# Two attention and feed-forward layers on one core: the opening is planned and placed anew

## The chip, the cores and the metric

The kernel runs on one core of a Trainium2 chip. The metric is the device time of one execution in microseconds (us). Three runs of the kernel before gave 1747.45, 1749.32 and 1751.42 us; the median, 1749.32 us, is the time before. A few figures come from one further execution that was recorded by the hardware profiler.

## The reference

```python
x = A_x                                            # 1 x 2048 x 512, bf16
x = x + _A_ref(_layernorm(x), A_wqkv, A_wo)        # attention: 32 heads of 16, full softmax
x = x + _B_ref(_layernorm(x), B_w1, B_w2)          # silu(x @ w1) @ w2, 512 -> 1792 -> 512
x = x + _A_ref(_layernorm(x), A_wqkv, A_wo)        # the same weights again
x = x + _B_ref(_layernorm(x), B_w1, B_w2)
```

The attention computes `softmax(q k^T / 4) v` over 2048 keys for each of 32 heads. The exponentials are 32 x 2048 x 2048 per layer; they are most of the work.

## The kernel before

**Units.** Scores are made in units of 128 keys by 512 queries of one head. Four heads share the TensorE array in row groups of 32 (`KT0` holds the keys of the first four, `KT1` of the next four, and so on; both come from one matmul group of a pair, `k_seq`). Scores go into two PSUM tiles in turn, `s3` of three banks and `s2` of two. ScalarE (ACT) exponentiates a whole tile in one instruction (`p<-s`). Where a bank and VectorE (DVE) are free, the planner gives a further unit to DVE (`spare`), which computes the exponential in four instructions (`v`, then three on `e`). `p` or `e` is then multiplied with V and a column of ones (`vaug`), which gives numerator and denominator together.

**A planner writes the order.** The program is made by a list scheduler that runs while the kernel is built. `Machine` keeps a model of the clock of each engine: `submit` queues an operation of ACT, DVE or SP with its cost; `track` finds what it depends on; `choice` picks the next one of an engine (priority -1 ahead of 0 ahead of 1, and an operation of higher priority is waited for by a fraction of a microsecond); `pump` emits all that begins before a given time; `pe` books a matmul. What is emitted stays in program order on its engine, so the model's times decide the order on the chip, but only semaphores decide when an instruction really starts. The tile framework (the follower of the program's order) adds those semaphores.

**The main loop** (in `stream`) tries at each step, in this order: scores (`emit_s`) if a score tile is free and its inputs are there; products with V (`pv_step`); a step of other matmuls (`fill_step`) from the lanes of `order()`; a dummy matmul (`dummy`). Dummies keep TensorE's clock up: one is made when the model's TensorE was busy for less than 0.66 (`FLOOR`) of the last 3.42 us (`WINDOW`).

**The opening.** The layer norm statistics of the first 1024 tokens are split between ACT and DVE. The lanes are `prep` (normalize a tile of 128 tokens into a `p` buffer), `turns` (transpose it on TensorE, copy it to `xt` by ACT or DVE, whichever the model has free first), `firsts` (keys of the first pair for two chunks of 512 tokens, then its early queries) and `values` (V tiles, `v_seq`). Eight tiles are turned so; the other eight are turned by DMA once scores run.

The early queries need a bound on the scores: the greatest absolute key of each row (`amaxp`, one reduction per chunk, then `amax`), put into the small matrices `E` by DVE, and `|q|` (`qa`). The matmul of `E` and `qa` subtracts the bound; its result is cast to `qt`, and then the first scores can be made. The names of the steps are thus, in order: `p` (normalized tile), `xt` (transposed), key matmuls, `amaxp`, `KT`, query matmuls, `qa`, `amax`, `E`, the matmul of `E` and `qa`, `qt`, scores `s`, exponential `p<-s`.

**Banks.** `g0` to `g2` (banks 0 to 2) live for the whole kernel. Banks 3 to 7 are `x0` to `x4` in the opening; at the first scores their pool is closed (`open_slots`), and `s3` takes banks 3 to 5, `s2` banks 6 and 7. Before the change a step in the opening takes whichever of the eight banks the model has free first, but once the query steps have begun, and always for those, only the first three. `slot_time` says when a score tile's banks are free, and scores are held while any of banks 3 to 7 is being filled.

**Around the exponential table.** ACT starts with the table set that has the square root. The first use of `Exp` loads another (`ACT_TABLE_LOAD`). Before the change a dummy `Exp` stands behind the first `qa`, which ACT computes with `Abs`. After the scores have begun (`started`), `qa` is always made by DVE.

**The end.** The last 256 tokens of the second layer can't be overlapped with more exponentials; `end_tokens` runs them with dummies of its own (`warm(11, ...)`) while their layer norm is computed.

In the profile most of ACT's, DVE's and TensorE's instructions carry the line of one of three helpers (L280, L419, L423), so they are told apart by the names of their tiles. Dummies are matmuls with `ident` as weights and `x_sb` as moving operand.

Of the kernel before, what the change touches and what calls it, by code (L numbers as in the profile page):

```python
# [10 lines left out]
ALU = mybir.AluOpType  # L11
# [21 lines left out]
class Machine:  # L33
# [13 lines left out]
    def __init__(self, tc):  # L47
        self.tc, self.on = tc, False
        self.regions, self.cache, self.grain = {}, {}, {}
        self.free = {"ACT": 0.0, "DVE": 0.0, "SP": 0.0}  # L50
        self.pending = {"ACT": [], "DVE": [], "SP": []}
        self.rows = [0.0] * 4
        self.mode, self.floor = None, 0.0
        self.busy = []

    def spans(self, ap):
# [32 lines left out]
    def track(self, op, reads, writes):  # L89
        deps = {}  # L90
        for ap in reads:
            known = self.regions.setdefault(ap.name, {})
            for w, _ in self.overlapping(ap):
                if w is not None:
                    deps[w] = 1
            for lo, hi in self.spans(ap):
                mine = known.setdefault((lo, hi), [None, []])
                if op.eng == "PE":
                    mine[1][:] = [o for o in mine[1] if o.eng != "PE"]
                mine[1].append(op)  # L100
        for ap in writes:
            known = self.regions.setdefault(ap.name, {})
            for lo, hi in self.spans(ap):
                for (a, b), (w, rs) in list(known.items()):
                    if a < hi and lo < b:
                        if w is not None:
                            deps[w] = 1
                        deps.update(dict.fromkeys(rs))
                        if lo <= a and b <= hi:
                            del known[a, b]  # L110
                known[lo, hi] = [op, []]
        deps.pop(op, None)
        return deps
# [110 lines left out]
    def pe(self, mode, row, cols, reads, writes, fn):  # L224

        op = Op("PE", 0.0, 0.0, (), None, 0)
        op.deps = self.track(op, reads, writes)
        if not self.on:
            op.end = 0.0
            return fn()  # L230
        for d in list(op.deps):
            self.force(d)
        if mode != self.mode:
            base = self.begins(mode)
            self.rows, self.mode = [base] * 4, mode
        rows = range(4) if row is None else (row,)
        self.floor = max(self.floor, self.ready(op))
        at = max(self.floor, *(self.rows[r] for r in rows))
        end = at + cols * self.COL
        for r in rows:  # L240
            self.rows[r] = end
        op.end = end + self.SEEN
        op.deps = ()
        if self.busy and at <= self.busy[-1][1] + 0.001:
            self.busy[-1][1] = max(self.busy[-1][1], end)
        else:
            self.busy.append([at, end])
        ins = fn()
        return self.tc.keep_in_program_order(ins)
# [48 lines left out]
class Seq:  # L298


    def __init__(self, steps, bank=True, when=None, lock=None, taken=None):
        self.steps, self.bank, self.when, self.lock, self.taken = steps, bank, when, lock, taken
        self.at, self.own = 0, None

    @property
# [40 lines left out]
def kernel(  # L346
# [106 lines left out]
    def bank_time(i):  # L453
        return INF if shut[i] else M.released(banks[i][:])

    def best_bank(every=True):
        return min(range(len(banks) if opening[0] and every else 3), key=bank_time)

    def take_bank(every=True):
        i = best_bank(every)  # L460
        assert not shut[i]
        shut[i] = True
        return i
# [167 lines left out]
    def k_seq(L, pr, c, when=None):  # L631

        def step(ct):
            def fn(g):
                mm(
                    g[:, :],
                    lhsT=wk_sb[:, ct, P * pr : P * (pr + 1)],
                    rhs=L.xnT[c][:, ct, :],
                    start=(ct == 0),
                    stop=(ct == CT - 1),  # L640
                )
                if ct < CT - 1:
                    return
                V.tensor_reduce(
                    out=amaxp[pr][:, c : c + 1], in_=g[:, :], axis=AX.X, op=ALU.max,
                    apply_absolute_value=True, prio=0 if started[0] else -1,
                )
                for par in range(2):
                    dst = KT[2 * pr + par][:, c * 512 : (c + 1) * 512]
                    if not started[0] and par == 0:  # L650
                        A.activation(
                            dst, g[:, :], ACT.Identity, bias=onescol[par], scale=headcol[par]
                        )
                    else:
                        V.tensor_scalar(
                            out=dst, in0=g[:, :], scalar1=headcol[par], scalar2=onescol[par],
                            op0=ALU.mult, op1=ALU.add, prio=0 if started[0] else 1,
                        )
                    L.k_made.add((2 * pr + par, c))
                used_xt(L, c)  # L660

            return fn

        return Seq([(step(ct), 512, lambda: [L.xnT[c][:]]) for ct in range(CT)], when=when)

    def v_seq(L, tt, cost=512, when=None):
        c = tt // 4

        def step(ct):
            def fn(g):  # L670
                at = tt % 4 * P
                mm(
                    g[:, :],
                    lhsT=L.xnT[c][:, ct, at : at + P],
                    rhs=wv_sb[:, ct, :],
                    start=(ct == 0),
                    stop=(ct == CT - 1),
                )
                if ct < CT - 1:
                    return  # L680
                dst = L.vaug[:, tt, 0 : 17 * H].rearrange("p (h e) -> p h e", e=17)[:, :, 0:DH]
                src = g[:, :].rearrange("p (h d) -> p h d", d=DH)
                L.v_made[tt] = evict(dst, src, 0 if started[0] else 1)
                used_xt(L, c)

            return fn

        return Seq([(step(ct), cost, lambda: [L.xnT[c][:]]) for ct in range(CT)], when=when)

    def new_vaug(n):  # L690
        vaug = keep([P, TT, VW], BF16, f"vaug{n}")
# [8 lines left out]
    def q_seq(L, c, pr, early=False, which=(0, 1), when=None):  # L700
# [3 lines left out]
        def step(ct):  # L704
            def fn(g):
# [29 lines left out]
                        )  # L735
                if ct < CT - 1:
                    return
                if not started[0]:
                    A.activation(qa[:], g[:, :], ACT.Abs)
                    if pr == 0:  # L740
                        M.submit(
                            "ACT", 1.5, 0.1, [qa[:]], [lnt[:, 0:1]],
                            lambda: nc.scalar.activation(lnt[:, 0:1], onescol[0], ACT.Exp),
                        )
                else:
                    V.tensor_scalar(
                        out=qa[:].bitcast(U16),
                        in0=g[:, :].bitcast(U16).rearrange("p (n h) -> p n h", h=2)[:, :, 1],
                        scalar1=0x7FFF, scalar2=None, op0=ALU.bitwise_and,
                    )  # L750
                used_xt(L, c)

            return fn
# [12 lines left out]
        def inputs(i):  # L766
# [3 lines left out]
        return Seq(  # L770
            steps + [(last(i), 512, inputs(i)) for i in range(len(which))],
            when=lambda: len(qt_ring.tiles) >= len(which) and (when is None or when()),
            lock="qa",
        )

    def drop_q(L, key):
# [358 lines left out]
    def stream(layers, before, values, side, last, second_half):  # L1135
# [295 lines left out]
        def step_of(lane, tp, ready=True):  # L1431


            if not lane.seqs:
                return None
            s = lane.seqs[0]
            if s.at == 0:
                if s.when is not None and not s.when():
                    return None
                if s.lock in Lane.locks:  # L1440
                    return None
                if s.bank and bank_time(best_bank(not s.lock)) > (tp + 0.02 if ready else 1e12):
                    return None
            if ready and M.written(*s.steps[s.at][2]()) > tp + 0.02 + (
                M.SWITCH if M.mode != "F" else 0.0
            ):
                return None
            return s

        def do_step(lane):  # L1450
            s = lane.seqs[0]
            if s.at == 0:
                if s.lock:
                    Lane.locks.add(s.lock)
                if s.bank:
                    s.own = take_bank(not s.lock)
            fn, cost, _ = s.steps[s.at]
            s.at += 1
            done = s.at == len(s.steps)
# [96 lines left out]
            return any(kt not in b.L.v_made for kt in range(k, n))  # L1556

        def fill_step(tp, s_at):
            urgent = not waiting or lacking() or short_of_v() or any(
                x[2].end is not None and x[2].end < tp - 2.0 for x in todo[:1]  # L1560
            )
# [104 lines left out]
    for at, t in (  # L1666
# [2 lines left out]
    ):  # L1669
        M.arrive(at, t)  # L1670
    M.free.update(ACT=4.0, DVE=2.5)
    M.WAIT = M.WAIT | {-1: 0.4}
    M.on = True
    HALF, ON_ACT = TT // 2, slice(3, 8, 4)
# [74 lines left out]
    def first_turn(tt):  # L1749
        c, tq = divmod(tt, 4)  # L1750

        def fn(g):
# [2 lines left out]
            dst = L1.xnT[c][:, :, tq * P : (tq + 1) * P]  # L1755
            if tt < HALF:
                to_transposed(room[tt], dst, g)
            else:
                by_dma(room[tt], dst)
            turned[c] += 1  # L1760
# [66 lines left out]
```

## Time and profile before

| | us |
|---|---|
| median of three runs | 1749.32 |
| profiled execution | 1750.5 |
| its span, first to last instruction | 1748.7 |
| ACT busy (98% of the span) | 1713.8 |
| DVE busy (93%) | 1629.3 |
| TensorE busy, matmuls (90%) | 1575.7 |
| first exponential of scores starts at | 21.49 |
| last exponential of scores starts at | 1723.40 |

The profile gives for each instruction its engine, line, operation and the tiles that it writes and reads (`out<-in`), its start and duration. In the timeline neighbouring instructions of a kind are merged: start, time from the start of the first to the end of the last, engine, line, operation, tiles, shape, count, and in brackets how long the engine had been idle before and on what it waited. PEld are TensorE's weight loads, which run beside the matmuls. A matmul's recorded time includes its way through the array, so the distance between neighbouring weight loads says better how fast TensorE works.

### The profile page before, as it was taken

How to read it: one execution, taken by the hardware profiler on the slowest of the kernel's cores; microseconds unless marked ns; L12 is line 12 of the kernel's file. 1: busy time of each engine (PE TensorE's matmuls, PEld its weight loads, DVE VectorE, ACT ScalarE, POOL GpSimd, SP SyncE). 2: the span in 40 equal slices, each digit the busy share in tenths (PEclk: the TensorE clock that was granted, in tenths of full speed). 3: DMA queues.
4: the chain of work that ended last, by engine and by line, in shares of the span. 5: the costliest groups of instructions: out<-in, count | busy, mean ns of one | idle time of the engine just before them, and what ended most of it. 6: DMA issues, size and time to landing. Idle time of an engine off the chain costs nothing.

```text
span 1748.7 us, 32237 instructions
## 1 busy us (share of the span) xinstructions
PE 1575.7 (90%) x12733; PEld 533.1 (30%) x12733; DVE 1629.3 (93%) x3165; ACT 1713.8 (98%) x1610; POOL 6.6 (0%) x20
## 2 busy tenths in 40 slices
PE   8899998999989999999989888989999898889988
PEld 2222222222222223334322222222222222333444
DVE  8999999999998999999999985979999999998995
ACT  8999999999999999999999999999999999999996
POOL 1000000000000000000000000000000000000000
PEclk9999999999999999999999999999999999999999
DMA  5100011000100001010010000100001000100100
GB/s 184 34 10 7 13 19 19 7 16 7 20 16 7 19 4 33 4 26 12 12 17 13 10 7 19 31 6 17 7 7 28 7 19 4 21 18 12 25 14 13
DMA packets 98088, 33.41 MB, mean 19 GB/s; under 512 B 89488, under 2 KB 97424, under 8 KB 97936
## 3 DMA queue, kind: packets, MB, share of 16 engines
q1 hardware_dynamic: 97936, 31.35, 8.2%
q8 instruction: 99, 1.62, 0.4%
q14 instruction: 53, 0.43, 0.1%
HBM read 7.86 MB, written 2.10 MB: 6 GB/s over the span
## 4 chain that ended last, share of the span: by engine, by line
ACT 44%; DVE 21%; PE 16%; issue 15%; DMA 3%; ACTq 0%; DVEq 0%
ACT p L280 41%; PE g L419 10%; DVE e L280 9%; PE s L419 5%; DVE v L280 4%; ACT t_sb L280 3%; DMA o<-oT 3%; DVE KT L280 2%; DVE hT L280 1%; DVE qt L280 1%; DVE amaxp L280 1%; DVE oT L280 1%; DVE vaug L280 0%; DVE qa L280 0%; DVE attn L280 0%
## 5 line engine op out<-in xcount | busy, mean ns | idle before, releaser
L280 ACT ACTIVATE p<-s 128x1536 bf16<-128x1536 f32 (+1 forms) x1446 | 1671.1, 1410 | 11.7 <-PE s L419 7.7
L419 PE MATMUL s<-qt,KT 32*128 32x512 bf16 (+1 forms) x4512 | 569.4, 339 | 108.8 <-ACT p L280 90.1
L419 PE MATMUL g<-p,vaug 128*32 128x512 bf16 (+1 forms) x4512 | 479.2, 344 | 17.8 <-ACT p L280 15.6
L419 PEld LDWEIGHTS <-KT 32*128 32x128 bf16 x5128 | 209.6, 91 | 623.2 <-issue 605.0
L280 DVE TENSOR_SCALAR v<-g 128x512 f32<-128x512 f32 x481 | 328.1, 682 | 23.8 <-PE g L419 18.6
L280 DVE SCALAR_TENSOR_TENSOR e<-e,v 128x512 uint16<-128x512 bf16 x481 | 325.4, 680 | 0.6
L280 DVE SCALAR_TENSOR_TENSOR e<-v,e 128x512 bf16<-128x512 uint16 x481 | 325.0, 680 | 0.7
L280 DVE SCALAR_TENSOR_TENSOR e<-v 128x512 bf16<-128x512 uint16 x481 | 322.5, 681 | 0.8
L419 PE MATMUL g<-wo_sb,ident 128*128 128x512 bf16 x681 | 210.6, 385 | 7.8 <-DVE v L280 5.3
L419 PEld LDWEIGHTS <-vaug 128*32 128x32 bf16 x5120 | 141.7, 95 | 220.5 <-issue 208.0
L419 PE MATMUL g<-qt,KT 32*128 32x512 bf16 (+1 forms) x608 | 185.4, 338 | 1.5 <-DVE KT L280 1.1
L419 PE MATMUL g<-e,vaug 128*32 128x512 bf16 (+1 forms) x608 | 173.0, 343 | 5.2 <-DVE e L280 2.5
L419 PE MATMUL g<-w_sb,hT 128*128 128x512 bf16 x448 | 131.2, 384 | 0.9 <-DVE hT L280 0.8
L419 PE MATMUL g<-xt,w_sb 128*128 128x512 bf16 x336 | 100.2, 387 | 9.3 <-DVE hT L280 6.5
L280 DVE SCALAR_TENSOR_TENSOR hT<-t_sb,g 128x512 bf16<-128x512 f32 x105 | 71.2, 678 | 21.2 <-ACT t_sb L280 20.9
L419 PEld LDWEIGHTS <-ident 128*128 128x128 bf16 x703 | 52.7, 98 | 112.3 <-issue 98.6
L280 ACT ACTIVATE t_sb<-g 128x512 f32<-128x512 f32 x105 | 82.4, 784 | 0.6 <-PE g L419 0.3
L280 DVE CAST oT<-g 128x512 bf16<-128x512 f32 (+1 forms) x94 | 55.6, 592 | 23.0 <-PE g L419 22.7
L419 PEld LDWEIGHTS <-hT 128*128 128x128 bf16 x568 | 41.8, 97 | 87.4 <-issue 69.7
L419 PEld LDWEIGHTS <-w_sb 128*128 128x128 bf16 x560 | 45.1, 98 | 68.9 <-issue 56.6
L280 DVE CAST qt<-g 128x512 bf16<-128x512 f32 x78 | 53.0, 680 | 2.9 <-PE g L419 2.8
L419 PE MATMUL g<-xt,wq_sb 128*128 128x512 bf16 x160 | 50.4, 390 | 1.9 <-DVE v L280 0.9
(128 smaller groups left out, 636.5 us busy)
## 6 DMA issues: line engine op xcount, KB each, us to landing
w_sb<-in_B_w_dram SPq DMA_DIRECT2D x2, 1792.0 KB, 13.9
x_sb<-in_A_x_dram SPq DMA_DIRECT2D x4, 512.0 KB, 7.0
out_dram<-x_sb SPq DMA_DIRECT2D x7, 256.0 KB, 2.1
o<-oT SPq DMA_TRANSPOSE x93, 2.4
xt<-hT SPq DMA_TRANSPOSE x48, 2.3
wk_sb<-in_A_wqkv_dram SPq DMA_DIRECT2D x1, 512.0 KB, 6.4
wq_sb<-in_A_wqkv_dram SPq DMA_DIRECT2D x1, 512.0 KB, 7.3
wv_sb<-in_A_wqkv_dram SPq DMA_DIRECT2D x1, 512.0 KB, 8.3
```

What stands on the lines that cost most here:

```text
L280: return self.m.submit(self.name, pitch, tail, aps, outs, lambda: fn(*args, **kw), prio)
L419: lambda: nc.tensor.matmul(out, lhsT=lhsT, rhs=rhs, **kw),
```

## The change

It has four parts, all of them in the opening or in the planner's picture of it.

1. The model books a matmul that begins before 10.4 us (`warm`) at 1.96 times its cost. Of the matmuls before that time only dummies are concerned.
2. `track` makes a read of a PSUM tile by ACT or DVE depend on earlier reads of it by the other of the two. This is in the model; the instructions and the semaphores of the tile framework are not changed by it, only the order of emission.
3. Keys and queries take banks 0 to 2, V tiles banks 6 and 7 until the score tiles exist, and banks 0 to 2 then. While scores have not begun, a filling step is not started if scores are due within 0.35 us.
4. The first `qa` is made by DVE, as the later ones are, and the dummy `Exp` stands behind the transposed copy of the eighth tile.

```diff
@@ Machine.__init__
-        self.mode, self.floor = None, 0.0
+        self.mode, self.floor, self.warm = None, 0.0, 0.0
@@ Machine.track, for each tile that is read
             for w, _ in self.overlapping(ap):
                 if w is not None:
                     deps[w] = 1
+            if op.eng != "PE" and ap.space == bass.MemoryType.PSUM:
+                for _, rs in self.overlapping(ap):
+                    deps.update((o, 1) for o in rs if o.eng not in (op.eng, "PE"))
@@ Machine.pe
-        end = at + cols * self.COL
+        end = at + cols * self.COL * (1.0 if at >= self.warm else 1.96)
@@ Seq.__init__
-    def __init__(self, steps, bank=True, when=None, lock=None, taken=None):
+    def __init__(self, steps, bank=True, when=None, lock=None, where=None):
@@ banks
-    def best_bank(every=True):
-        return min(range(len(banks) if opening[0] and every else 3), key=bank_time)
-
-    def take_bank(every=True):
-        i = best_bank(every)
+    def best_bank(where=None):
+        if s_slots or where is None and not opening[0]:
+            where = range(3)
+        return min(where or range(len(banks)), key=bank_time)
+
+    def take_bank(where=None):
+        i = best_bank(where)
@@ k_seq, v_seq, q_seq: what their Seq is given
+        k_seq: where=range(3)      v_seq: where=(6, 7)      q_seq: where=range(3)
@@ q_seq, after the last query matmul
-                if not started[0]:
-                    A.activation(qa[:], g[:, :], ACT.Abs)
-                    if pr == 0:
-                        M.submit(
-                            "ACT", 1.5, 0.1, [qa[:]], [lnt[:, 0:1]],
-                            lambda: nc.scalar.activation(lnt[:, 0:1], onescol[0], ACT.Exp),
-                        )
-                else:
-                    V.tensor_scalar(
-                        out=qa[:].bitcast(U16),
-                        in0=g[:, :].bitcast(U16).rearrange("p (n h) -> p n h", h=2)[:, :, 1],
-                        scalar1=0x7FFF, scalar2=None, op0=ALU.bitwise_and,
-                    )
+                V.tensor_scalar(
+                    out=qa[:].bitcast(U16),
+                    in0=g[:, :].bitcast(U16).rearrange("p (n h) -> p n h", h=2)[:, :, 1],
+                    scalar1=0x7FFF, scalar2=None, op0=ALU.bitwise_and,
+                )
@@ step_of, do_step
-                if s.bank and bank_time(best_bank(not s.lock)) > (tp + 0.02 if ready else 1e12):
+                if s.bank and bank_time(best_bank(s.where)) > (tp + 0.02 if ready else 1e12):
...
-                    s.own = take_bank(not s.lock)
+                    s.own = take_bank(s.where)
@@ fill_step
+            if not started[0] and s_at < tp + 0.35:
+                return False
@@ beginning of the planned part
     M.free.update(ACT=4.0, DVE=2.5)
+    M.warm = 10.4
@@ first_turn
             if tt < HALF:
                 to_transposed(room[tt], dst, g)
+                if tt == HALF - 1:
+                    M.submit(
+                        "ACT", 1.5, 0.1, [dst], [lnt[:, 0:1]],
+                        lambda: nc.scalar.activation(lnt[:, 0:1], onescol[0], ACT.Exp),
+                    )
```

## The prediction

> **What bounds the kernel now.** I began with the page: its span and its busy lines say which engine is full, and the slices say where it is not.
>
> ```profile
> span 1748.7 us, 32237 instructions
> PE 1575.7 (90%) x12733; PEld 533.1 (30%) x12733; DVE 1629.3 (93%) x3165; ACT 1713.8 (98%) x1610; POOL 6.6 (0%) x20
> ```
>
> ScalarE (ACT) is busy for all but 34.9 us. Where those 34.9 us lie is answered by the table of stretches (columns: length, then busy time of PE, PEld, DVE, ACT, POOL):
>
> ```profile
> 0.00:21.49 21.49, 15.31 (x83) 7.07 (x83) 13.90 (x44) 14.19 (x34) 6.58 (x20) 1.00 0.95 323
> 21.49:60.00 38.51, 35.38 (x228) 9.82 (x227) 37.91 (x92) 37.91 (x34) 0.00 (x0) 1.00 0.23 59
> ...
> 1726.00:1748.70 22.70, 17.88 (x108) 10.45 (x108) 9.69 (x18) 6.59 (x10) 0.00 (x0) 0.90 0.04 12
> ```
>
> 7.3 us lie before the first exponential at 21.49, 16.1 us in the tail, and 11.5 us are spread over the 1704.5 us between. So the time is: start (21.49) + ACT's queue, nearly without a hole, + tail (22.7). A change of the beginning moves the total by what it moves the first exponential, one for one, and beyond that only through what it does to the length of ACT's queue. The third view is the timeline of the opening:
>
> ```profile
> 10.23 1.23 PEld L419 LDWEIGHTS <-ident 128*128 128x128 bf16 x6 [0.28 <-issue]
> ...
> 11.79 0.83 PE L423 MATMUL x<-ident,p 128*128 128x128 bf16 x12
> 12.21 1.56 ACT L280 COPY xt<-x 128x512 bf16<-128x512 bf16 x3 [1.35 <-PE x L423]
> ...
> 16.88 0.81 DVE L280 TENSOR_SCALAR KT<-x,cols 128x512 bf16<-128x512 f32 x1 [0.85 <-ACT KT L280]
> ...
> 17.46 0.60 ACT L280 ACTIVATE qa<-g 128x512 bf16<-128x512 f32 x1
> 17.60 0.68 DVE L280 TENSOR_REDUCE amaxp<-g 128x1 f32<-128x512 f32 x1
> ...
> 18.07 1.28 ACT L743 ACT_TABLE_LOAD   x1
> ...
> 19.67 0.68 DVE L280 CAST qt<-g 128x512 bf16<-128x512 f32 x1
> ...
> 20.27 0.68 DVE L280 CAST vaug<-x 128x512 bf16<-128x512 f32 x1
> ...
> 21.00 0.39 PE L419 MATMUL s<-qt,KT 32*128 32x512 bf16 x3 [0.61 <-DVE vaug L280]
> ...
> 21.49 9.15 ACT L280 ACTIVATE p<-s 128x1536 bf16<-128x1536 f32 x8 [0.94 <-PE s L419]
> ```
>
> To be seen: PE still works off dummies until 11.58, though the first normalized tile was there at 9.69 + 0.35 = 10.04; DVE's KT stands 0.85 behind ACT's read of the same bank, and amaxp of the second key chunk stands behind that, though its matmuls (15.54 to 16.56) were long done; the first scores wait 0.61 for a V eviction after qt. Each of the four parts of the change goes at one of these.
>
> **Dummies at the cold rate.** The 20 dummies before the transposes (20 weight loads of ident) are issued 0.43 apart until 10.23 and 0.216 apart after (six loads in 1.23). The planner booked all of them at 0.218, so its PE clock ran ahead of the chip's. With 0.218 x 1.96 = 0.427 each and the unchanged rule (fill 0.66 of 3.42 us = 2.26 us), I count by hand: six dummies from 4.8 to 7.4, none until the first slides out of the window at 8.6, four more to 10.3, where the tile is due: 10 in place of 20. On the chip nothing holds PE in the planned gap, so they end at 4.73 + 10 x 0.427 = 9.00. The transposes then start when the tile lands, at about 10.15, not 11.58: 1.43 gained on PE. ACT can't use all of it: its own p and a sel run to 10.87 (10.59 + 0.28), so its copies start at 10.87, not 12.21: 1.34. From there by the rows: 1.56 for three copies, 0.52 for the fourth, 0.77 for four small constants, 0.60 for the last copy: 14.32, where it was 15.49. The second chunk's key matmuls follow at 14.4 and end at 15.3 (they took 0.86 of issue from 15.54 to 16.40).
>
> **Readers of a bank in a row.** The model now makes a read of a PSUM tile wait for earlier readers on other engines, which is what the 0.85 shows the chip doing. It adds no instruction. DVE will be given amaxp of chunk 1 before KT of chunk 0. It can start at 15.3 + 0.2 = 15.5, not 17.60. From amaxp to the last E operation took 17.60 to 19.04, 1.44, so E stands at 16.94 and not 19.04: 2.1 of lead. Elsewhere the rule binds nothing new: after the opening DVE alone reads key banks, and tanh's bank has its ACT reader ahead of DVE's already through t_sb.
>
> **Abs moves to DVE, the exp table moves ahead.** qa was ACT's 0.60 at 17.46, beside DVE's work. On DVE it takes 0.68 (the other 39 qa average 681 ns) and now stands in the row behind E, since the E operations have the higher priority: 16.94 to 17.62. That is the full 0.68 on the path. Queued behind it: KT of the odd head (0.81 each, twice) and V evictions. The table load (1.28, with its dummy activation 0.20) goes behind the last copy, 14.32 to 15.80; KT of both chunks on ACT follow to about 17.3 (0.78 and 0.68 of pitch). That is 1.8 ahead of the new qt, so the load costs nothing; if that cover were gone it would cost at most its 1.48. In the old place it cost nothing either: ACT idled for 0.94 before its first exponential. No second load is expected, as ACT went from exp to vaug's cast and back at 19.96 to 21.49 without one.
>
> **qt and the first scores.** The E matmul (0.39) runs from 17.65 to 18.05; DVE, free at 17.62, will fill the wait with a KT (0.81), to 18.43; qt follows to 19.1, the scores start at 19.15, and the exponential 0.49 later: 19.65. Against 21.49 that is 1.84 earlier.
>
> **V tiles in banks 6 and 7.** Before, one V eviction in an x bank held the scores for 0.61. The trace can't show whether the scores' new tile waits for all five old banks or only for the three it covers. Bounds: 0.6 gained if the wait goes; 0.7 lost if a second eviction (0.68) stands in front. My chain to 19.65 has no such wait; in the row's own order, an eviction right behind qt, it comes back at 0.6: 20.25. I take the middle, 19.9, since V tiles still sit in banks that the score tiles take over, and ACT, idle after 17.3, can take some of the evictions: the start moves by 21.49 - 19.9 = 1.6. The new guard (no filling step within 0.35 us of the scores) and the fixed sets of three banks for keys and queries add no work; they can delay a V tile, whose first reader comes 3.3 us behind the scores (24.34 against 21.00).
>
> **The rest of ACT's queue.** Eight exponentials of 20 units in 9.15 us make 0.46 us a unit. DVE takes 481 of the units (the costliest groups of the page: four instructions of 0.68 each). Every unit that changes sides moves the end by 0.46. What DVE brings over the start (two KT, 1.6 us, less than one unit's 2.7) is worth 0.3. But the planner places every later step anew from the shifted state. DVE's idle time between 60 and 1726 is about 99 us, so its time does not fix the split; free banks and the backlog rule do. The profile excludes neither sign: I take zero, and as bounds 8 units either way (3.7 us, one in sixty of the 481). The tail has one more term. Its eleven dummies run at half clock:
>
> ```profile
> 1727.23:1730.64 3.41, 3.35 (x8) 1.19 (x9) 2.04 (x8) 1.94 (x4) 0.00 (x0) 0.50 0.00 0
> ```
>
> The transposes behind them start at 1731.53, where their input (first of two writes in 0.73 from 1730.28) was there at about 1730.7: 0.8 can come back if the slow stretch falls elsewhere, and as much or 1.7 (half of 3.41) be lost if it falls on the hidden matmuls. I take zero.
>
> **Sum.** The profiled execution took 1750.5 (span 1748.7 and 1.8 around it): 1750.5 - 1.6 = 1748.9. The median of the runs shown is 1749.3, so there the same step gives 1747.7.
>
> **Rivals.**
> The start moves and the split or the tail falls kindly: 1.6 + 7 units x 0.46 = 4.8, or 1744.5. For it: 99 us of idle DVE. Against: nothing in the change aims there. 0.22.
>
> More units stay on ACT, and the end is slower. Mechanism: at the start DVE now owes two KT and the V evictions, its backlog is over the 3.0 us at which the planner offers it no unit, and the order that follows finds a bank free less often. Each lost unit costs 0.46; from four the gain of 1.6 is gone, at twelve (2.5% of 481) it is +3.9: 1753.2. For it: DVE is 98% busy between 21.49 and 60 (37.91 of 38.51), so there is nothing to catch up with. Against: that stretch is 2% of the span. 0.15.
>
> The clock stays low. Ten dummies fill 4.3 us where twenty kept PE busy up to the transposes, and PE then idles from 9.0 to 10.15. In this run 5.5 us of unbroken dummies were needed (4.73 to 10.23). If 4.3 do not do, the four key, four key, four query matmuls and the E matmul run at 0.427 in place of 0.216, 13 x 0.21 = 2.7, while the transposes (0.26 a tile, then 0.5) still hide behind copies of 0.52. The start is then 1.1 later than before: 1750.4. It decides itself at the weight loads after 10.2. 0.13. The Trainium skill, TensorE: Matmul & The Clock Gate, Part 1, says that full clock is granted after one busy window of some 3.4 us on a free-running grid, and Part 4 that transposes don't count as busy in the same way; by that rule ten dummies suffice for most positions of the grid and fail for some, and the trace's 5.5 us agree with a grid, since its first window was only partly filled. That the rule speaks against thinner dummies is why I do not leave this rival out.
>
> **How the numbers follow.** The forecast, 1747.7 with the rest of the queue unmoved, has 0.50. What a measurement of this kernel can tell from no change is about 0.2%, 3.5 us. Faster by more: the kind rival 0.22 and 0.04 from the forecast's edge; slower by more: the unkind one 0.15 and 0.01 of the cold clock; between lie 0.58. The range reaches 4.8 + 1 below and 2.9 above the median: 1743.5 to 1752.2.
>
> **What would show it.** Right: 10 or 11 weight loads of ident before the transposes, these at 10.1 to 10.3; amaxp of the second chunk ahead of any DVE KT; qa on DVE right behind E; the table load between the last xt copy and ACT's KT; first exponential between 19.3 and 20.3; the count of v on DVE within 8 of 481. Wrong: loads of wk_sb 0.43 apart after 10.3, ACT idle between its KT, scores still waiting for vaug, or an end that moves by other than the start did.

## The result

The changed kernel took 1745.14 us (median of 13 runs, 1741.14 to 1748.49), the kernel before 1748.25 us beside it (13 runs, 1744.97 to 1751.59). The ratio is 0.9974, 95% interval 0.9964 to 0.9984: faster by 0.26%, which is 4.5 us of 1748. The ratio compares the means; the two medians are 3.1 us apart. In a second set of runs on another chip the ratio was 0.9951 (0.9936 to 0.9967).

The page of the changed kernel's profiled execution (1745.14 us):

```profile
span 1743.4 us, 32282 instructions
...
PE 1568.3 (90%) x12750; PEld 530.6 (30%) x12750; DVE 1630.2 (94%) x3168; ACT 1713.3 (98%) x1611; POOL 6.6 (0%) x20
```

The span is 5.3 shorter; ACT's work is the same to 0.5 us. The table of stretches is cut at this kernel's first scores (19.57) and behind its last exponential (1719.73 to 1720.53). It gives the length, then the busy time of PE, PEld, DVE, ACT and POOL, the mean granted clock, and the share and rate of the DMA:

```profile
0.00:19.60 19.60, 12.37 (x74) 5.92 (x74) 13.24 (x44) 14.47 (x35) 6.56 (x20) 1.00 0.94 319
19.60:60.00 40.40, 38.49 (x245) 10.88 (x244) 39.91 (x96) 39.53 (x35) 0.00 (x0) 1.00 0.28 74
...
1722.00:1743.40 21.40, 16.51 (x108) 9.99 (x108) 9.56 (x18) 6.46 (x10) 0.00 (x0) 0.97 0.04 12
```

From the instructions' times of the two profiles: the first exponential starts at 20.06 (before 21.49, 1.4 earlier), the time from the first to the last one is 1699.67 (before 1701.91, 2.2 shorter), and from there to the end it is 23.6 (before 25.3, 1.7 shorter). So the start carries a quarter of the profiled gain. Units on DVE: 482 (before 481). Between the start of the first and the end of the last exponential ACT was idle for 9.6 us (before 11.4) and busy for 1690.9 (before 1691.8). The opening in the timeline:

```profile
10.38 1.52 PEld L426 LDWEIGHTS <-p 128*128 128x128 bf16 x20 [2.12 <-DVE p L283]
...
11.13 1.52 ACT L283 COPY xt<-x 128x512 bf16<-128x512 bf16 x3
...
14.38 1.28 ACT L1765 ACT_TABLE_LOAD   x1
...
15.58 0.69 DVE L283 TENSOR_REDUCE amaxp<-g 128x1 f32<-128x512 f32 x1 [0.68 <-PE g L422]
...
15.78 1.43 ACT L283 ACTIVATE KT<-g,cols 128x512 bf16<-128x512 f32 x2
...
16.91 0.69 DVE L283 TENSOR_SCALAR qa<-g 128x512 uint16<-128x512 uint16 x1
...
17.51 0.80 DVE L283 TENSOR_SCALAR KT<-g,cols 128x512 bf16<-128x512 f32 x1
...
18.23 0.68 DVE L283 CAST qt<-g 128x512 bf16<-128x512 f32 x1
...
18.93 0.59 ACT L283 CAST vaug<-x 128x512 bf16<-128x512 f32 x1 [0.68 <-PE x L422]
...
19.57 0.39 PE L422 MATMUL s<-qt,KT 32*128 32x512 bf16 x3 [0.68 <-ACT vaug L283]
...
20.06 4.62 ACT L283 ACTIVATE p<-s 128x1536 bf16<-128x1536 f32 x4 [0.55 <-PE s L422]
```

To be seen: PE now waits 2.12 for the first normalized tile, where that tile had waited for PE; the second amaxp stands ahead of every KT; qa follows E on DVE, a KT fills the wait before qt, and the scores still wait 0.68 for a V eviction, now ACT's.

Where the rest came from shows when the finished units (ACT's and DVE's together, 4096) are counted in both traces. The changed kernel leads by 1.4 us at unit 3, trails by 2.5 at unit 2048 (870 us), trails by 0.2 at unit 2304 (981 us), and leads by 5.4 at unit 2816 (1203 us). That one step of 5.6 us is more than the whole gain between the first and the last exponential (2.2); elsewhere the changed kernel loses ground, 3.9 us up to unit 2048 and 1.7 behind unit 2816. In that stretch the second layer takes over. Its groups, first before, then after (mean of one, idle time ahead of them and who ended it):

```profile
L280 ACT ACTIVATE p<-s 128x1024 bf16<-128x1024 f32 (+1 forms) x187 | 217.4, 1368 | 3.9 <-PE g L419 2.4 <-PE s L419 1.2
```

```profile
L280 DVE TENSOR_SCALAR v<-g 128x512 f32<-128x512 f32 x49 | 33.4, 682 | 5.1 <-PE g L419 4.5
```

```profile
L283 ACT ACTIVATE p<-s 128x1536 bf16<-128x1536 f32 (+1 forms) x186 | 215.3, 1464 | 0.4 <-PE g L422 0.4
```

```profile
L283 DVE TENSOR_SCALAR v<-g 128x512 f32<-128x512 f32 x53 | 36.4, 686 | 1.8 <-PE g L422 1.5
```

ACT stood for 3.9 us there before and for 0.4 after, and DVE took 53 units instead of 49: 3.5 + 4 x 0.46 = 5.3, which is about the step from 0.2 behind to 5.4 ahead. Nothing in the change aims at this place. The step is not one execution's: the six other profiles of the changed opening, from the experiments below, have it too (5.0 to 7.0 us, with at most 0.9 us of such holes and 52 or 53 units on DVE). Of ACT's holes in the kernel before, 2.3 us lie in two stretches of half clock, at 1027.5 and 1143.6; whether the clock made them or the same sparse work made both is not shown.

The tail's eleven dummies now run at full clock, issued in 2.26 us, where the eleven loads of before went from 1727.69 to 1731.42:

```profile
1723.35 2.26 PEld L422 LDWEIGHTS <-ident 128*128 128x128 bf16 x11
```

### The profile page after: what moved, and what is told of

It is laid out like the page before. It is cut to its first block, busy times and chain, and to the rows that moved or that the text cites. A ratio compares the mean times of both kernels' runs of the same rounds, so it can differ in the third digit from the quotient of the medians.

```text
span 1743.4 us, 32282 instructions
## 1 busy us (share of the span) xinstructions
PE 1568.3 (90%) x12750; PEld 530.6 (30%) x12750; DVE 1630.2 (94%) x3168; ACT 1713.3 (98%) x1611; POOL 6.6 (0%) x20
## 4 chain that ended last, share of the span: by engine, by line
ACT 50%; DVE 19%; issue 16%; PE 12%; DMA 3%; ACTq 0%; SPq 0%; DVEq 0%
ACT p L283 46%; DVE e L283 8%; PE g L422 7%; PE s L422 4%; DVE v L283 4%; ACT t_sb L283 3%; DMA o<-oT 3%; DVE KT L283 1%; DVE hT L283 1%; DVE oT L283 1%; DVE amaxp L283 1%; DVE qt L283 1%; DVE qa L283 0%; DVE x_sb L283 0%; DVE attn L283 0%
## 5 line engine op out<-in xcount | busy, mean ns | idle before, releaser
L422 PE MATMUL g<-p,vaug 128*32 128x512 bf16 (+1 forms) x4514 | 476.5, 343 | 14.1 <-ACT p L283 13.0
## 6 DMA issues: line engine op xcount, KB each, us to landing
w_sb<-in_B_w_dram SPq DMA_DIRECT2D x2, 1792.0 KB, 14.1
```

The costliest lines, as they stand in the source:

```text
L422: lambda: nc.tensor.matmul(out, lhsT=lhsT, rhs=rhs, **kw),
```

## The experiments

Ratios are to runs of the kernel before in the same set, with 95% intervals. "First exponential" is from the one profiled execution of each; x lands at 4.7 to 5.0 in them, except where noted. "From landing" counts the same from where x lands; a star marks profiles in which TensorE's clock was at half for some of the work between the dummies and the first scores. "At equal clock" is an estimate: the time in us above or below the kernel before on the same chip, with both brought to the same mean granted clock by one straight line through all 194 runs that list a clock (-920 us for the whole of the clock); the 95% intervals of its entries are 0.7 to 1.1 us either way. It also takes out what a kernel itself does to the clock.

| kernel | ratio | first exponential | from landing | units on DVE | at equal clock |
|---|---|---|---|---|---|
| changed kernel, first set | 0.9974 (0.9964 to 0.9984) | 20.06 | 15.12 | 482 | no clocks for before |
| changed kernel, again | 0.9951 (0.9936 to 0.9967) | 20.88 | 16.13* | 482 | -6.0 |
| 24 late matmuls | 0.9947 (0.9932 to 0.9962) | 23.30 | 18.59 | 482 | -6.6 |
| 24 early matmuls | 0.9930 (0.9912 to 0.9947) | 20.92 | 16.17* | 482 | -9.5 |
| x lands late | 0.9979 (0.9964 to 0.9995) | 23.23 | 15.22 | 482 | -2.6 |
| changed, placed with 0.201 | 0.9961 (0.9946 to 0.9976) | 21.61 | 16.72* | 481 | -5.8 |
| changed, placed with 0.199 | 0.9963 (0.9949 to 0.9977) | 20.09 | 15.19 | 482 | -6.6 |
| before, placed with 0.201 | 0.9987 (0.9976 to 0.9999) | 20.59 | 15.86 | 483 | -1.2 |
| part 1 alone | 1.0007 (0.9994 to 1.0019) | 22.25 | 17.36* | 480 | 0.8 |
| part 4 alone | 0.9951 (0.9934 to 0.9968) | 19.93 | 15.14 | 484 | -6.2 |
| parts 1, 3, 4 | 1.0003 (0.9991 to 1.0015) | 20.74 | 15.99 | 483 | -2.8 |
| parts 1, 2, 4 | 1.0002 (0.9990 to 1.0014) | 20.09 | 15.37 | 480 | -0.4 |
| parts 1, 2, 3 | 1.0052 (1.0033 to 1.0070) | 21.17 | 16.52* | 476 | 1.1 |

**Is the end moved by what the start is moved?** First the changed kernel again, and with 24 matmuls in front of the first transposes that the planner doesn't book.

> The changed kernel once more, as the ruler for the other runs of this set. The theory that the first exponential's lead is all (1.6 us of 1748) expects 0.9991 of the kernel before; the theory that the order placed anew behind the start gave about as much again expects 0.997 to 0.998, as on record.

> The changed kernel with 24 matmuls more in front of the first transposes that the planner does not know of: the order of everything else is that of the changed kernel, only the start comes later, by 4 to 7 us (24 at 0.216 to 0.427 from where the ten dummies end, less the 1.1 us in which PE was idle). Theory one for one (ACT's queue has no hole that could take up a late start): the end comes later by what the first exponential comes later, 4 to 7 us, within 1 us. Rival (engines have slack and catch up): less than half of that arrives at the end, 0 to 3 us.

```diff
+            if tt == 0:
+                for _ in range(24):
+                    tc.keep_in_program_order(
+                        nc.tensor.matmul(
+                            g[:, :], lhsT=ident[:, :], rhs=x_sb[:, 0, :], start=True, stop=True
+                        )
+                    )
             if tt < HALF:
                 to_transposed(room[tt], dst, g)
```

The start came 2.4 to 3.2 later (23.30; 4 to 7 had been expected), and the time was the same: medians 1743.09 and 1743.26. As it stood, the rival had won. The instructions of ACT and DVE and their order are the same in both. But the two traces, instruction by instruction, keep the 3.24 unchanged from the first exponential to 66 us and lose it later at separate places. DVE's wait for `o`, a tile that SP transposes by DMA, was one of them: at 294.6 DVE waited 1.2 in the changed kernel and not in the late one.

```profile
L628 SPq DMA_TRANSPOSE o<-oT x93: 1168/1190/2427, 38.0 to 1711.5; - x93
```

Most transposes are issued in 1.19 us, some in up to 2.4. All long ones (over 1.5: 10 of 179 in the changed kernel, 7 in the late one) have a packet of the instruction queue between 1.5 us ahead of their issue and 2.6 behind it; of all 179, 60 and 54 have, so most with such a packet are not long. The additional matmuls change which ones are long: counted in their order on SP's queue, 9 of the changed kernel's 10 long ones are long again in its second profile and 8 with late data (below; TensorE's stream is the same), but none of them with 24 matmuls more; the late and the early run share 5 of their 7 and 8. So the 24 additional matmuls did two things: they delayed the start, and they moved everything behind them in TensorE's instruction stream, after which other transposes were long. Two runs separate these.

> The changed kernel with the 24 unplanned matmuls put where TensorE waits for x anyway (128 columns, before 4.7 us) instead of in front of the transposes: TensorE's stream is as long as in the run with 24 late matmuls, and all that follows stands at the same place in it, but the start is not delayed (first exponential near 20, not 23.3). Theory that the late run took its 2.4 to 3.2 us back because its longer stream meets fewer slow transposes and weight-clock stretches: 1740 to 1741, 2.4 to 3.2 below the late run. Rival (the start's time does not reach the end): 1743, like the late run.

```diff
     M.on = True
+    for _ in range(24):
+        tc.keep_in_program_order(
+            nc.tensor.matmul(
+                banks[1][:, 0:P], lhsT=ident[:, :], rhs=ident[:, :], start=True, stop=True
+            )
+        )
```

> The changed kernel with the loads of wk and wq put ahead of the first loads of x: no engine's instructions or their order change, but x lands some 2 to 3.5 us later (two loads of 512 KB more ahead of it) and with it the whole opening. Theory one for one: the end comes 2 to 3.5 us later than that of the changed kernel, as the first exponential does. Rival from the run with 24 late matmuls (a late start is taken up by slack behind it): the end moves by under 1 us.

```diff
+    def load_w(w, at):
+        nc.sync.dma_start(w[:], A_wqkv[:, at : at + D].rearrange("(ct p) f -> p ct f", p=P))
+
+    load_w(wk_sb, D)
+    load_w(wq_sb, 0)
     load_x(0)
     load_x(1)
-    for w, at in ((wk_sb, D), (wq_sb, 0), (wv_sb, 2 * D)):
-        nc.sync.dma_start(w[:], A_wqkv[:, at : at + D].rearrange("(ct p) f -> p ct f", p=P))
+    load_w(wv_sb, 2 * D)
```

With a stream of the same length and no delay, the first exponential came 2.38 earlier than in the late run (20.92), and the ratio is 0.9930 against 0.9947: 0.17%, 3.0 us, for 2.4 of start. With an unchanged stream and x landing at 8.01 instead of 4.75 to 4.95, the first exponential came 2.4 to 3.2 later (23.23), and the ratio is 0.9979 against 0.9951: 0.28%, 4.9 us. These ratios are from different sets, each to the kernel before beside it, and the interval of such a difference is some 0.22% either way. So the first pair fits one for one and doesn't exclude nothing; the second excludes nothing and fits one for one. Together they give 0.23% (0.15% either way) for about 2.6 us of start, or 0.15%. But the second pair hangs on which ratio of the changed kernel is taken: with the 0.9974 of the first set, 0.05% is left. By the ratios alone the rival is not out.

The clocks settle it. At equal clock, late data costs 3.3 us (1.3 either way) and the late run is 2.9 (1.5 either way) behind the early one: both exclude nothing and fit one for one. The profiles agree: between the changed kernel and late data, which have the same instructions of ACT and DVE in the same order, the first exponential moves by 3.17 and the span by 3.19, though their distance wanders between 2.0 and 5.0 in the middle; between the early and the late run it is 2.38 and 2.81.

What the longer stream gave by itself is the early run against the changed kernel with the same start (20.92 and 20.88): 0.9930 against 0.9951, 3.7 us; their intervals overlap a little, but at equal clock it is 3.5 us (1.5 either way). That its cause is the transposes was seen at single places and not isolated. The early run has the lowest ratio of all; it beats the kernel before clearly and the changed kernel by that margin.

**What does placing anew give?** A single constant of the model is moved by 1 ns from the first scores on.

> The changed kernel with one constant of the model changed from the first scores on (a matmul's result is taken to be seen after 0.201 instead of 0.200 us): the opening is the same, all that follows is placed anew. Theory that where the planner happens to place things decides some us: the end moves by up to 3 us either way against the changed kernel though the start does not. Rival (placing anew is worth nothing): within 1 us of the changed kernel.

> As the run with 0.201, with 0.199: a second draw of the order behind the same start. The same two theories: up to 3 us either way, or within 1 us of the changed kernel.

> The kernel before with the model's constant at 0.201 from the first scores on: the same opening, all behind it placed anew. Theory that what the change gained beyond its start is a draw of the placement, and that the kernel before has a slow draw: 3 to 6 us below the kernel before. Rival (the changed opening leaves a state that is better to go on from): within 1.5 us of the kernel before.

```diff
     def second_half():
         halves_asked[1] = True
+        M.SEEN = 0.201      # 0.199 in the other run
```

DVE's order leaves the changed kernel's at 878 us (0.201) and at 164 us (0.199), that of the kernel before at 630 us. The changed opening gave 0.9961 and 0.9963, the old one 0.9987: differences of the order of 0.1% by 1 ns, upward behind the new opening and downward behind the old. Those of the new opening are within the intervals (the medians are 2.1 and 2.6 us above the changed kernel's, and at equal clock the three are within 0.8 us), so neither of their two theories is out. The old opening's second draw came 2.3 us (0.13%) lower, not 3 to 6 and not within 1.5, but its interval, 0.2 to 4.2 us, reaches into both ranges. Three draws behind the new opening lie lower than two behind the old one. Whether this holds of the opening or of five draws stays open; below, two kernels with most of the new opening do not lie lower by the ratio.

One of these profiles also shows a rival of the prediction at work. The opening's order is the changed kernel's, yet its first exponential is 1.55 later (21.61). The columns are those of the table of stretches:

```profile
9.00:12.50 3.50, 2.11 (x24) 1.29 (x24) 3.03 (x12) 3.47 (x12) 0.00 (x0) 1.00 1.10 348
12.50:15.90 3.40, 3.40 (x18) 1.92 (x17) 1.29 (x4) 2.47 (x7) 0.00 (x0) 0.50 1.09 375
```

The clock (column behind POOL) was full, and after a stretch in which PE was busy for 2.11 of 3.50, mostly with transposes, it fell to half for 3.4 us. Such a stretch doesn't always cost the clock: in the changed kernel's first profile PE was busy for 1.78 of the 3.41 us from 7.99, in the one with 0.199 for 2.27 of the 3.41 from 9.52, and the clock stayed full. What decides it stays open. In the early run it fell at 11.0, and in the second run of the changed kernel, by the spacing of its weight loads (0.4 up to 13.81), it was not full before 14.1. Counted from x's landing, the first exponential of this opening came at 15.12, 15.19 and 15.22 in three profiles at full clock and at 16.13, 16.17 and 16.72 in these three. The old opening has two profiles, 15.86 (full clock from 8.5) and 16.78 (from 10.3).

**Which part does it?** One part alone, then all but one.

> The kernel before with the first part alone (dummies booked at the cold rate). Theory of the prediction: the transposes start 1.3 us earlier and the first exponential 1.0 to 1.4 earlier than 21.5; the end by the same, with up to 3 us of placement either way. Rival (the clock stays low with ten dummies): transposes 0.107 apart and a first exponential no earlier than 21.5.

The diff is part 1 of the change on the kernel before. The transposes started 1.6 earlier from x's landing (5.51 against 7.08), and the first exponential came later than before, 22.25:

```profile
16.28 0.78 ACT L280 ACTIVATE KT<-g,cols 128x512 bf16<-128x512 f32 x1 [1.00 <-DVE amaxp L280]
18.53 0.78 ACT L280 ACTIVATE KT<-x,cols 128x512 bf16<-128x512 f32 x1 [1.48 <-DVE amaxp L280]
```

The time is the rival's, but the clock did not stay low with ten dummies: it was full from 8.9 and fell to half from 12.3 to 15.8. The lead is also lost behind DVE's readers (ACT's two KT wait 1.00 and 1.48 for amaxp). How much each took is not separated; the changed kernel with 0.201, at half clock in the same place, has 16.72 from x's landing against 17.36 here. The end did not move measurably.

> The kernel before with the fourth part alone (first qa on DVE, exp table behind the last transposed copy). Theory of the prediction: by itself it costs, 0.7 us of qa on DVE's row in front of qt and up to 1.5 of table load in front of ACT's KT: first exponential at 22 to 23. Rival (moving the load off the place in front of the first scores is where the change gains): first exponential at 20.0 to 20.5.

Part 4 on the kernel before. First exponential 19.93, ratio 0.9951: the rival's direction, just under its range. From x's landing that is 15.14, and 0.72 earlier than the old opening at full clock (15.86). The table load does not cost its 1.48, it re-orders:

```profile
14.70 1.28 ACT L1753 ACT_TABLE_LOAD   x1
...
16.10 0.76 ACT L280 ACTIVATE KT<-x,cols 128x512 bf16<-128x512 f32 x1
```

```profile
15.14 0.80 DVE L280 TENSOR_SCALAR KT<-x,cols 128x512 bf16<-128x512 f32 x1
15.86 0.68 DVE L280 TENSOR_REDUCE amaxp<-g 128x1 f32<-128x512 f32 x1
```

While ACT loads the table, DVE reads the first chunk's bank for its KT ahead of ACT, with no wait of 0.85, and the second amaxp follows at 15.86. Which half of part 4 did it, the load's place or qa on DVE, was not run apart.

> Parts one to three without the fourth: qa stays on ACT, the exp table load behind it. Theory of the prediction: qa no longer stands in DVE's row, so the first exponential comes up to 0.7 earlier than in the changed kernel, 19.3 to 20.0. Rival (from the run of part four alone): the load of 1.28 then stands in front of ACT's V evictions, which hold the scores, and the first exponential comes at 20.7 to 21.5.

Parts 1 to 3. First exponential 21.17, in the rival's range:

```profile
18.75 0.68 DVE L283 CAST qt<-g 128x512 bf16<-128x512 f32 x1
19.34 1.28 DVE L283 CAST vaug<-x 128x512 bf16<-128x512 f32 x2
```

```profile
20.68 0.39 PE L422 MATMUL s<-qt,KT 32*128 32x512 bf16 x3 [2.31 <-DVE vaug L283]
```

ACT loads its table from 17.97 to 19.25, so two V evictions go to DVE behind qt and the scores wait for them. The clock has a share too: it was not full before 13.3, and qt starts 0.8 later from x's landing than in the changed kernel (14.10 against 13.28). The end is 0.52% later, much more than the start. DVE took 476 units, and ACT stood idle for 20.1 us between the first and the last exponential, 13.5 of them in stretches of half clock (4.95 in one wait at 378, in a stretch of 10.24). The mean granted clock of these runs is 0.985, that of the kernel before 0.994; at equal clock only 1.1 us of 9 are left.

> Parts one, three and four, without readers of a bank kept in a row in the model. Theory of the prediction: amaxp of the second key chunk falls behind KT's readers again, and the first exponential comes 1 to 2 us later than in the changed kernel, 21 to 22.5. Rival (from the run of part four alone): the early table load by itself puts ACT's KT behind amaxp, and the first exponential stays at 20 to 20.6.

Parts 1, 3 and 4:

```profile
15.52 0.81 DVE L280 TENSOR_SCALAR KT<-g,cols 128x512 bf16<-128x512 f32 x1 [0.84 <-ACT KT L280]
16.25 0.68 DVE L280 TENSOR_REDUCE amaxp<-g 128x1 f32<-128x512 f32 x1
```

KT waits 0.84 for ACT's read again and the second amaxp comes behind it. From x's landing the first exponential is 0.87 later than in the changed kernel (15.99 against 15.12), near the theory's lower end; 20.74 by the span lies between the two ranges.

> Parts one, two and four, without banks of their own for V tiles and without the guard. Theory of the prediction (V tiles sit in banks that the score tiles take over either way): first exponential as in the changed kernel, 19.9 to 20.6. Rival (the banks take a wait of 0.6 away): 20.7 to 21.3.

Parts 1, 2 and 4: 20.09, as the theory had it; the banks of their own move the start by 0.25 from x's landing (15.37 against 15.12). So parts 1, 2 and 4 have nearly the changed kernel's start and no gain at the end (1.0002); parts 1, 3 and 4 have lost the new start (15.99, against 15.86 of the old opening at full clock) and gain nothing either (1.0003).

## Why the prediction was right, and where not

The direction and the range held (1745.14 in 1743.5 to 1752.2); the range ran from 5.8 us below the kernel before to 2.9 above and so held no change too: to lie inside it says little. The direction came right in good part for another reason than the forecast's, since parts 1, 2 and 4 have the start and no gain. The size was under-estimated: 0.26% is 4.5 us, and 1.6 was forecast. The time of the rival in which split and tail fall kindly (1744.5) is what came; it had 0.22. Its mechanism came in part: the tail was kind, but the split moved by one unit and not by seven. Two of the signs that the prediction named as wrong came too: the scores still wait for vaug, and the end moved by other than the start (5.4 against 1.4 in the profiles).

**Dummies: right in the order, over-priced in the gain.** Ten matmuls, the last one done at 8.76 (forecast 9.00), transposes at 10.39. With x landing 0.24 later in this profile, the copies (forecast 10.87, measured 11.13) stand where they were put, and the steps behind them come close: second amaxp 15.5 and 15.58, qa 16.94 and 16.91, qt 18.43 and 18.23, exponential 19.9 and 20.06. But the start of the old opening was read from one profile, whose clock became full only at 10.3. Its transposes began 7.08 from x's landing; in the two other profiles with the old dummies (before with 0.201, part 4 alone), full from 8.5 and 8.6, they began at 6.16 and 6.20, and in those with ten dummies at 5.42 to 5.53. So about 0.9 of the 1.43 that the prediction gained on PE was that one profile's late clock.

**V tiles: the middle was taken, and the whole wait stayed,** 0.68, now for ACT. That the exponential still came where it was forecast is luck: from x's landing, qt started 0.44 earlier than forecast (13.28 against 13.72), which made up for it.

**The table load at no cost: right for the sum, wrong for what it does.** The two profiles agree that it is hidden. But part 4 alone gives the whole start (15.14 from landing, the changed kernel 15.12 to 15.22 at full clock) and the whole gain at the end (-6.2 us at equal clock, the changed kernel -6.0), and without it the scores wait 2.31 for V evictions. The prediction priced where the load stands on ACT and not what DVE does in the meantime, nor that in its old place it would drive V evictions onto DVE once the scores come earlier.

**The clock: the chance of 0.13 was far too low.** In three of six profiles of this opening the clock was at half in the middle of it. The price was over-estimated: 1.0 to 1.5 against the mean of the other three, not 2.7, since one stretch at half clock covers only a part of the matmuls that the rival counted. Ten dummies fill 4.27 us, so they cover a whole 3.41 us from end to end for only a quarter of its possible places (0.86 of 3.41), not for most as the prediction put it; yet in seven of the nine profiles with ten dummies alone (not in the changed kernel's second one and in parts 1 to 3) the clock became full from them, in the first one from a stretch (4.58 to 7.99) in which they began 0.4 late. So the start was mis-sized too: over the profiles at hand it moves by about 0.6 (means 15.76 of six and 16.32 of two from x's landing), at full clock by 0.7, not 1.6. That the two profiles on which prediction and result rest show 1.43 is luck of their clocks. The Trainium skill, TensorE: Matmul & The Clock Gate, Part 1, gives a busy window of some 3.4 us on a free-running grid as the condition for full clock; the half-clock stretches of 3.4 us and their changing places agree with that. The table of the same part lets the clock fall after an idle window; here it fell, in the run shown above, with no gap over 1.13 (9.26 to 10.39) and transposes behind it, and the measurement decides. That transposes count for less, which the prediction took in, is not borne out by parts 1 to 3: there the clock became full at 13.29, after 3.41 us in which PE was busy for 3.13 and worked off 24 transposes and one other matmul.

**The rest of the queue taken as zero: the term that was mis-sized most.** Between 981 and 1203 us it gave 5.3, and over the kernels whose first exponential comes within 1 us of the changed one's the ratio ranges from 0.9930 to 1.0003, 13 us. The bound of 8 units (3.7 us) covered only the split; ACT's own holes were left out of it. Between the first and the last exponential they make 4.8 us (early run) to 20.1 (parts 1 to 3) in the fourteen profiles, while ACT's work there differs by 5.2. Why an order has fewer holes was not isolated.

**Tail: the 0.8 came back**, and some more, in this profile (23.6 from the last exponential's start to the end); in the seven of the changed opening it is 23.6 where no half-clock stretch falls between 1715 and 1740, and 24.6 to 25.3 in the three where one does.

**One for one: right** with the same instructions in the same stream (3.3 and 2.9 us at equal clock for 2.4 to 3.2 and 2.4 of start, each 1.3 to 1.5 either way); a comparison between different programs can hide it.

## What to carry to other kernels

In a program that a planner orders, a change of the opening buys two things, the start and a new order of everything behind it, and the second can be several times the first. Price the first from the timeline of several profiles, since one profile's clock can be worth more than the change; give the second its own width from the holes of the bottleneck engine and from the split between engines, and measure it by moving a constant by next to nothing. Compare runs at the same granted clock as well as by their ratio. To test what a delay costs, delay the data and leave the instruction streams alone.

## What the runs showed of the hardware

The time of one execution goes with its mean granted clock: over 35 runs of the kernel before, a correlation of -0.89 and -1019 us for the whole of the clock. One half-clock stretch of 3.41 us takes 3.41 / 2 / 1749 = 0.00098 of it, so it goes with about 1.0 us (an estimate from that slope; which of the two drives the other is not shown). In the profiles an execution had four to eight stretches of half clock, one to five times 3.41 us long, many of them at other places in another execution of the same kernel; the correlation (0.89 squared, 0.79) goes with most of the spread among these runs, 1745.41 to 1755.86. In the stretches between the first and the last exponential ACT itself stood idle for 0.4 to 1.1 us per 3.41 us of half clock.

Of the 179 transposes by DMA in an execution 5 to 16 took over 1.5 us of SP's queue, up to 2.75, instead of 1.19. All of these had a packet of the instruction queue close by, but so had 47 to 65 others that were short. Forty-eight more TensorE instructions at the start (24 matmuls with their weight loads) changed which transposes were long.
